# Attention with hashed buckets and two dense layers: value products with 65 weight columns, a host-made projection table, new planner tables

## The chip, the cores and the metric

One core of a Trainium2 chip runs the whole program. The metric is the device time of one execution in microseconds. TensorE does the matrix products (PE in the profile; PEld its weight loads), VectorE is DVE, ScalarE is ACT, GpSimd is POOL, and SyncE (SP) issues nearly all DMA transfers.

## The reference

```python
def _attn_ref(q, k, v, proj):          # 2 x 8 heads, 768 rows, 64 columns
    q_bits, k_bits = (q @ proj > 0), (k @ proj > 0)      # 6 bits each
    mask = q_bucket[:, :, :, None] == k_bucket[:, :, None, :]
    scores = np.where(mask, scale * q @ k.T, -1e9)
    attn = np.exp(scores - scores.max(-1, keepdims=True))
    return (attn / (attn.sum(-1, keepdims=True) + 1e-9)) @ v
x = (1536 tokens, 512)
x = leaky_relu(x @ w_in) @ w_out       # 512 -> 2048 -> 512, slope 0.01
h = x @ w_in2;  out = (h * cos(h)) @ w_out2
```

Everything is float32.

## The kernel before, in words

Products are made in pairs of rounded parts: each operand is split into a high part (a rounded copy, by ScalarE) and a low part (what is left, by a subtraction on POOL or DVE), and high x high, high x low and low x high are summed in PSUM.

There are 16 heads. One head's queries and keys, transposed, stand as a 128 x 768 tile (raw). `hi` and `lo` split it, `bits_mm` (line 277) multiplies it with the signed projection table PB, `bits_wr` (line 283) turns the signs into rows of the tile AT, scaled so that rows of different buckets get a large negative score. `at_dma` copies parts of AT between partitions. `max_mm` (293) forms the scores of 128 rows by 768 at a time, and `max_red` (299) their maximum on DVE; after six of them `row_mm`, `row_fin` and `row_dma` (303 to 313) write the maxima as one more row of AT, beside a row of -1 that `minus_one` loads by DMA (454). `qk` (370, 371) then forms scores that have the maximum already subtracted, `exp` and `exp_cv` (377 to 388) take the exponential on ScalarE and its rounded copy, `exp_lo` (392) subtracts; LO says which of DVE and POOL does it. `pv` (405) multiplies with V, six key blocks, three pairs of parts and two halves of 384 columns, 36 products a head, and `pv_e` (397) opens the sum with two products that add the epsilon and the case of rows without a partner. The old weights are 128 columns: 64 of V and 64 of ones (VH) or zeros (VL), so that 64 rows of the result hold the row sum; even and odd heads share the ones and so have V above or below. `evac` (412) copies the result out, row sums go through a DMA, `recip` (419), a DMA to DRAM and a broadcast back (`lc_dma`, `dr_dma`, `rr_dma`), and `xmul` (430) divides. Every four heads V is loaded (325), split (331, 335), and summed over its rows by products with ones (`sum_v`, 342; 65 weight columns, 256 streamed).

The dense layers (`Moe`, lines 664 to 742) follow: each of two layers takes 48 steps of 12 input and 12 output products of 512 columns; the last four steps divide one output block into two halves of 256 (`columns`, 708). The integer weights are made into two float parts by seven steps per chunk (`Weights.stages`, lines 581 to 592, on ScalarE, DVE and POOL); eight chunks are begun during heads 12 to 15.

The order of nearly all this up to the twelfth dense step is written by a planner (`Plan.order`, line 116). It runs a list of operations in a model of five queues (PE, DVE, ACT, POOL, SP): each has a cost (COST), what it must follow, and a place in a ring of buffers. The queue that can start first takes the operation that can start first there, and among those that could start at the same moment, the one with the least key. The key is the head's position (6 a head) plus KEY of the kind, or FIX of kind and head. CHUNK_KEY does the same for the weight chunks. Program order on each engine is what results. The first loads and constants (lines 209 to 251) stand outside the planner, ahead of it; `zeros` and `v_ones` are two operations of POOL in it. Costs model the duration of each; products before 22 us count 1.9 times as long.

Of the kernel before, what the change touches and what calls it, by code (L numbers as in the profile page):

```python
# [49 lines left out]
}  # L50
CHUNK_KEY = (132.0, 106.0, 116.9, 111.2, 249.3, 102.4, 235.2, 115.5)

COST = dict(
    load=0.5, hi=0.83, d2=0.55, d3=0.55, lo=1.87, dl=0.55, bm=1.06, bw=1.1, db2=0.7, db1=0.55,
    mm=0.351, mr=0.953, rt=0.12, fl=0.55, dr=0.75, de=1.3, neg=0.65, qk=0.702, ex=0.81, cv=0.84, subV=0.95, subG=1.87,
    pe=0.351, pv=0.702, pw=0.351, ev=0.83, lc=0.55, rc=0.18, dw=0.45, rr=0.55, xm=1.85, xh=0.83, xl=1.87,
    vload=0.6, vh=0.83, vl=1.87, sv=1.37, sh=0.75, sl=0.4,
    wload=0.4, w0=1.11, w1=0.69, w2=0.69, w3=1.15, w4=1.15, w5=1.06, w6=2.4,
    hi0=0.52, lo0=0.52, k2=0.83, idt=0.5, bm0=1.0, bw0=0.69, kb0=0.52,
    mi=2.73, ga=0.6, gm=0.68, gh=0.63, glV=0.65, glG=1.3, mo=2.73, ye=0.65,  # L60
)
# [22 lines left out]
BM = 96 + 2 * NB  # L84
# [10 lines left out]
class Plan:  # L95
# [799 lines left out]
```

## Time and profile before

| | us |
|---|---|
| timed runs, median of 3 | 791.51 |
| lowest and highest | 790.81, 791.82 |
| profiled execution, first to last instruction | 789.9 |
| PE busy | 772.2 (98%) |
| DVE, ACT, POOL busy | 472.9, 435.1, 408.9 |

The profiled execution has a span and no separate device time of its own; the timed runs lie 0.9 to 1.9 us above the span. Since products are pipelined, PE's busy time counts a product's record, which overlaps with the next one's, and is no measure of how densely products follow each other. That is read from the distance between starts, or from a merged piece of the chain of waits: its length divided by its count.

### The profile page before, as it was taken

How to read it: one execution, taken by the hardware profiler on the slowest of the kernel's cores; microseconds unless marked ns; L12 is line 12 of the kernel's file. 1: busy time of each engine (PE TensorE's matmuls, PEld its weight loads, DVE VectorE, ACT ScalarE, POOL GpSimd, SP SyncE). 2: the span in 40 equal slices, each digit the busy share in tenths (PEclk: the TensorE clock that was granted, in tenths of full speed). 3: DMA queues.
4: the chain of work that ended last, by engine and by line, in shares of the span. 5: the costliest groups of instructions: out<-in, count | busy, mean ns of one | idle time of the engine just before them, and what ended most of it. 6: DMA issues, size and time to landing. Idle time of an engine off the chain costs nothing.

```text
span 789.9 us, 9962 instructions
## 1 busy us (share of the span) xinstructions
PE 772.2 (98%) x3660; PEld 666.1 (84%) x3660; DVE 472.9 (60%) x599; ACT 435.1 (55%) x630; POOL 408.9 (52%) x263
## 2 busy tenths in 40 slices
PE   5999999999998999999999999999999999999998
PEld 3999999999888888888888888888888888888886
DVE  6656777777597875256366275357546738743333
ACT  3687777877778744243243233366556645644432
POOL 8777675666575634255345346747615433532211
PEclk9999999999999999999999999999999999999999
DMA  6553543542613622032022013112203200000012
GB/s 179 134 129 84 147 96 92 137 104 65 197 32 132 219 107 107 1 107 90 18 107 75 32 54 108 53 41 75 98 1 107 107 1 1 0 1 1 0 54 107
DMA packets 24329, 63.20 MB, mean 80 GB/s; under 512 B 7596, under 2 KB 11620, under 8 KB 20184
## 3 DMA queue, kind: packets, MB, share of 16 engines
q1 hardware_dynamic: 24136, 62.43, 26.0%
q8 instruction: 29, 0.48, 0.3%
q14 instruction: 20, 0.16, 0.1%
q10 hardware_dynamic: 144, 0.13, 0.0%
HBM read 46.21 MB, written 3.19 MB: 63 GB/s over the span
## 4 chain that ended last, share of the span: by engine, by line
PE 92%; DVE 3%; ACT 2%; DMA 2%; issue 1%; POOL 0%; SPq 0%; DVEq 0%; ACTq 0%; POOLq 0%
PE h L664 33%; PE y L706 33%; PE pv L405 11%; PE st L293 4%; PE st L370 4%; PE st L371 4%; PE st L277 2%; PE st L342 1%; DMA raw<-in_qk_dram 1%; PE pv L397 1%; DMA sums<-yx 1%; DVE mx L299 0%; ACT st L385 0%; DVE wsc L591 0%; ACT phi L377 0%
## 5 line engine op out<-in xcount | busy, mean ns | idle before, releaser
L695 POOL TENSOR_TENSOR gl<-gf,gh 128x512 fp32r<-128x512 f32 x88 | 136.2, 1548 | 261.1 <-ACT gh L689 188.7
L706 PE MATMUL y<-gh,at 128*128 128x512 f32 x576 | 177.0, 388 | 0.0
L664 PE MATMUL h<-XH,at 128*128 128x512 f32 x576 | 142.3, 389 | 0.0
L664 PEld LDWEIGHTS h<-XH,at 128*128 128x128 f32 x576 | 108.1, 188 | 22.4
L706 PEld LDWEIGHTS y<-gh,at 128*128 128x128 f32 x576 | 108.0, 188 | 22.4
L299 DVE TENSOR_REDUCE mx<-st 128x1 fp32r<-128x768 f32 x96 | 90.3, 953 | 37.1 <-PE st L293 35.3
L706 PE MATMUL y<-gl,at 128*128 128x512 f32 x288 | 111.8, 388 | 0.0
L392 POOL TENSOR_TENSOR plo<-pf,phi 128x768 fp32r<-128x768 f32 x43 | 81.3, 1894 | 56.1 <-ACT phi L388 49.3
L671 ACT ACTIVATE gf<-h 128x512 f32<-128x512 f32 x48 | 28.7, 597 | 139.8 <-PE h L664 135.8
L681 DVE TENSOR_TENSOR gf<-h,gf 128x512 f32<-128x512 f32 x48 | 33.2, 691 | 108.2 <-ACT gf L671 108.0
L675 ACT ACTIVATE ki<-h 128x512 int32<-128x512 f32 x48 | 28.7, 598 | 105.1 <-PE h L664 105.1
L676 DVE SCALAR_TENSOR_TENSOR gf<-ki,h 128x512 f32<-128x512 int32 x48 | 33.0, 687 | 75.1 <-ACT ki L675 75.1
L664 PE MATMUL h<-XL,at 128*128 128x512 f32 x288 | 77.0, 389 | 0.0
L370 PE MATMUL st<-at 77*128 77x384 f32 x192 | 67.0, 349 | 3.3 <-DVE plo L392 1.3
L371 PE MATMUL st<-at 128*128 128x384 f32 x192 | 65.1, 339 | 0.0
L585 POOL TENSOR_TENSOR at<-wsc,at 128x1024 fp32r<-128x1024 f32 x24 | 59.1, 2462 | 9.6 <-ACT at L592 9.6
L664 PEld LDWEIGHTS h<-XL,at 128*128 128x128 f32 x288 | 54.1, 188 | 11.2
L706 PEld LDWEIGHTS y<-gl,at 128*128 128x128 f32 x288 | 54.0, 188 | 11.1
L689 ACT ACTIVATE gh<-gf 128x512 fp32r<-128x512 f32 x96 | 60.0, 625 | 3.0 <-DVE gf L681 1.5
L706 PE MATMUL y<-gh,wx 128*128 128x512 f32 x192 | 58.7, 387 | 0.0
L685 DVE SCALAR_TENSOR_TENSOR gf<-gf,h 128x512 f32<-128x512 f32 x48 | 32.9, 686 | 41.7 <-ACT gf L684 41.7
L392 DVE TENSOR_TENSOR plo<-st,phi 128x768 fp32r<-128x768 f32 x53 | 50.3, 952 | 10.5 <-ACT st L385 9.1
(105 smaller groups left out, 1452.1 us busy)
## 6 DMA issues: line engine op xcount, KB each, us to landing
wrvh<-in_w_dram SPq DMA_DIRECT2D x16, 1024.0 KB
wrvl<-in_w_dram SPq DMA_DIRECT2D x16, 1024.0 KB
at<-at SPq DMA_DIRECT2D x63, 192.0 KB
raw<-in_qk_dram SPq DMA_DIRECT2D x15, 384.0 KB
vraw<-in_v_dram SPq DMA_DIRECT2D x4, 768.0 KB
yx<-dr SPq DMA_DIRECT2D x16, 192.0 KB
out_dram<-ys SPq DMA_DIRECT2D x6, 256.0 KB
out_dram<-yx SPq DMA_DIRECT2D x5, 256.0 KB
```

What stands on the lines that cost most here:

```text
L299: V.reduce_max(mx[n][:, t:t + 1], mps.pop((n, t))[:, :, 0:HS], axis=AX.XY)
L370: T.matmul(o, at[0:R76 + 1, 2, kc], at[0:R76 + 1, 0, COL[h]], start=True, stop=False)
L371: T.matmul(o, at[:, 3, kc], at[:, 1, COL[h]], start=False, stop=True)
L392: (V if LO[n][k] == "V" else G).tensor_tensor(halves(plo[n, k]), pf.pop((n, k)), halves(f32(phi[n, k])), op=ALU.subtract)
L405: T.matmul(ot[n][:, h, 0:HS], w, x[:, COL[h]], start=False, stop=(k == C - 1 and part == 1))
L585: G.tensor_tensor(lf, sc, f32(hf), op=ALU.subtract)
L664: self.tc.nc.tensor.matmul(ps, w[:, 0, k], x[:, k, cols], start=(j == 0), stop=(j == 3 * KT - 1))
L676: nc.vector.scalar_tensor_tensor(g, ki, -TWOPI, ps, op0=ALU.mult, op1=ALU.add)
L681: nc.vector.tensor_tensor(g, ps, g, op=ALU.max)
L689: self.tc.nc.scalar.activation(gh, self.gs[s], AF.Copy)
L695: (nc.vector if s < GLV else nc.gpsimd).tensor_tensor(gl, g, f32(gh), op=ALU.subtract)
L706: self.tc.nc.tensor.matmul(self.half(e, c), w[:, 1, e], x[:, c], start=(j == 0 and i == 0), stop=(j == GRP - 1 and i == 2))
```

## The change

The weights of a value product are 65 columns (64 of V and one of ones or zeros) for every head, so the row sum is row 64 of the result in every head; SV, the evacuation and the divide follow this layout, and odd heads are divided from partitions 0 to 63 into 64 to 127, with a tile of their own (rr1) for the reciprocals. The projection table is laid out on the host with a table of its signs beside it (128 x 218 values), and both are loaded on ScalarE's queue with the constants; DVE makes PB by three operations. The halves of head 0 become operations of the planner (`ld0`), the first on SP's queue. The row of -1 comes out of the bit write, so `minus_one` goes. The memsets of E and SV move from POOL to DVE. `behind` is new in the planner: the operation may start once the other has started, not ended; the loads of heads use it. Its tables are made anew: 432 entries of FIX for kind and head where there were 49, other costs, keys, and a time that passes between an operation's end and its result (TAIL). In the diff, lines of context and repeated small edits are left out, and the entries of FIX.

```diff
-    load=-181, hi=20, d2=-40, d3=51, lo=-43, dl=-14, bm=-37, bw=7, db2=-47, db1=-61, mm=-8, mr=34, rt=-30,
-    fl=60, neg=1, dr=-74, de=-45, qk=0.72, ex=-7, cv=31, sub=-14, pe=101, pv=39, pw=-4, ev=19, lc=42, rc=40,
-    dw=-34, rr=-34, xm=69, xh=55, xl=-23, vload=71, vh=3, vl=-6, sv=-9, sh=55, sl=-32, wload=94, w0=62, w1=48,
-    w2=-14, w3=49, w4=-27, w5=96, w6=43, mi=4, ga=-51, gm=-35, gh=121, gl=-54, mo=84, ye=-9,
+    load=-1402.5, hi=-438.67, d2=-769.89, d3=-983.25, lo=-187.57, dl=-709.62, bm=-17.82, bw=-521.3, db2=-1419.35,
+    db1=211.01, mm=-7.13, mr=-1162.47, rt=-1.18, fl=-477.39, dr=117.38, de=366.66, qk=1.53, ex=-447.6, cv=-866.91,
+    sub=-567.77, pe=1936.57, pv=585.55, pw=-477.86, ev=-342.96, lc=1443.25, rc=-983.12, dw=-594.71, rr=1500.38,
+    xm=912.21, xh=-1553.48, xl=-197.89, vload=3019.65, vh=1673.03, vl=1768.56, sv=1402.49, sh=1294.13, sl=1341.39,
+    wload=1281.32, w0=-319.38, w1=1137.97, w2=2068.37, w3=552.4, w4=1061.17, w5=950.32, w6=884.09, mi=40.93,
+    ga=153.93, gm=-1034.74, gh=808.61, gl=283.21, mo=-543.31, ye=-455.08,
...
-CHUNK_KEY = (132.0, 106.0, 116.9, 111.2, 249.3, 102.4, 235.2, 115.5)
+CHUNK_KEY = (484.78, 3377.12, -1208.89, 3288.78, 2056.81, -547.14, -95.7, -707.94)
-    load=0.5, hi=0.83, d2=0.55, d3=0.55, lo=1.87, dl=0.55, bm=1.06, bw=1.1, db2=0.7, db1=0.55,
-    mm=0.351, mr=0.953, rt=0.12, fl=0.55, dr=0.75, de=1.3, neg=0.65, qk=0.702, ex=0.81, cv=0.84, subV=0.95, subG=1.87,
-    pe=0.351, pv=0.702, pw=0.351, ev=0.83, lc=0.55, rc=0.18, dw=0.45, rr=0.55, xm=1.85, xh=0.83, xl=1.87,
-    vload=0.6, vh=0.83, vl=1.87, sv=1.37, sh=0.75, sl=0.4,
-    wload=0.4, w0=1.11, w1=0.69, w2=0.69, w3=1.15, w4=1.15, w5=1.06, w6=2.4,
-    hi0=0.52, lo0=0.52, k2=0.83, idt=0.5, bm0=1.0, bw0=0.69, kb0=0.52,
-    mi=2.73, ga=0.6, gm=0.68, gh=0.63, glV=0.65, glG=1.3, mo=2.73, ye=0.65,
+    load=0.6, hi=0.735, d2=0.6, d3=0.6, lo=1.81, dl=0.56, bm=1.053, bw=1.117, db2=0.85, db1=0.58,
+    mm=0.349, mr=0.87, rt=0.06, fl=0.43, dr=0.78, de=1.55, qk=0.704, ex=0.705, cv=0.735, subV=0.875, subG=1.81,
+    pe=0.347, pv=0.683, pw=0.341, ev=0.69, lc=0.6, rc=0.1, dw=0.42, rr=0.56, xm=1.8, xh=0.735, xl=1.8,
+    vload=0.65, vh=0.735, vl=1.8, sv=1.39, sh=0.785, sl=0.45,
+    wload=0.4, w0=1.03, w1=0.6, w2=0.6, w3=1.13, w4=1.13, w5=0.96, w6=2.36,
+    ld0=0.6, hi0=0.58, lo0=0.47, k2=0.735, idt=0.48, bm0=0.53, bw0=0.69, kb0=0.52,
+    mi=2.72, ga=0.495, gm=0.605, gh=0.537, glV=0.602, glG=1.3, mo=2.72, ye=0.55,
-LAT = dict(P=0.06, V=0.04, A=0.04, G=0.1, Q=0.03)
+LAT = dict(P=0.06, V=0.04, A=0.04, G=0.06, Q=0.03)
+TAIL = dict(P=0.16, V=0.09, A=0.1, G=0.05, Q=0.0)
+COLD = 18.0
...
-BM = 96 + 2 * NB
+BM = 96 + 2 * NB + 1
+DV = D + 1
...
-    def add(self, name, e, kind, key, fn, after=(), take=None, give=(), cost=None, moe=False):
+    def add(self, name, e, kind, key, fn, after=(), take=None, give=(), cost=None, moe=False, behind=()):
+        ahead = [self.index[d] for d in behind if d in self.index]
-                  cost=COST[kind] if cost is None else cost, out=[], left=len(deps), moe=moe, before=[], place=0)
+                  cost=COST[kind] if cost is None else cost, out=[], left=len(deps) + len(ahead), moe=moe, before=[], place=0, behind=[], ahead=ahead)
+        for d in ahead:
+            d["behind"].append(it)
...
-            if e == "P" and t < 22:
+            if e == "P" and t < COLD:
...
-            end = t + c
+            for o in it["behind"]:
+                o["left"] -= 1
+                o["at"] = max(o.get("at", 0.0), t)
+                if o["left"] == 0:
+                    ready[o["e"]].append(o)
+            end = t + c + TAIL[e]
-                end = wire + 0.8
+                end = wire + 1.1
...
-                o["at"] = max(o.get("at", 0.0), end + LAT[o["e"]] * (o["e"] != e or e == "Q"))
+                o["at"] = max(o.get("at", 0.0), end + LAT[o["e"]] if e != "P" or o["e"] != e else t + c)
...
-        SV = [con.tile([128, 4, 128], F32R, name=f"sv{i}") for i in range(2)]
-        ring("svt", [128, 2, 2, 64], F32R)
+        SV = [con.tile([128, 4, DV], F32R, name=f"sv{i}") for i in range(2)]
+        ring("svt", [128, 4, D], F32R)
...
-        RR, XX = (YX[:, i * S:(i + 1) * S] for i in (2, 3))
+        RR, XX = [YX[0:64, 2 * S:3 * S], rr1], YX[:, 3 * S:4 * S]
+        raw = {}
+        COL = [slice(h * HS, (h + 1) * HS) for h in range(2)]
+        px = con.tile([128, 2 * BM], F32, name="px")
-        pj = con.tile([128, NB], F32, name="pj")
-        Q.dma_start(pj[0:64], proj)
-        Q.dma_start(pj[64:128], proj)
-        raw = {0: plan.tiles["raw"][0]}
-        COL = [slice(h * HS, (h + 1) * HS) for h in range(2)]
-        for c in COL:
-            Q.dma_start(raw[0][:, c], qkt[0, 0][:, c])
-        Q.dma_start(cs, cst)
+        A.dma_start(px, proj)
+        A.dma_start(cs, cst)
-        ph_ = con.tile([128, NB], F32R, name="ph_")
-        pl_ = con.tile([128, NB], F32, name="pl_")
-        for t in PB:
-            V.memset(f32(t), 0.0)
-        V.tensor_copy(ph_, pj)
-        V.tensor_tensor(pl_, pj, f32(ph_), op=ALU.subtract)
-        for t, p in zip(PB, (f32(ph_), pl_)):
-            for s in range(2):
-                for j in range(2):
-                    rows, c0 = slice(64 * s, 64 * s + 64), 64 + 32 * s + j * NB
-                    V.tensor_scalar(t[rows, c0:c0 + NB], p[rows], 1.0 if s == j else -1.0, None, op0=ALU.mult)
-        neg = con.tile([C, 128], F32, name="neg")
-        G.memset(neg, -1.0)
-        ones = con.tile([128, 65], F32R, name="ones")
+        ones = con.tile([128, DV], F32R, name="ones")
-        def zeros():
+        for i in range(2):
+            V.memset(f32(E[i]), 0.0)
+            V.memset(f32(SV[i]), 0.0)
+        signed = px[:, 0:BM]
+        V.tensor_tensor(signed, signed, px[:, BM:], op=ALU.mult)
+        V.tensor_copy(PB[0], signed)
+        V.tensor_tensor(PB[1], signed, f32(PB[0]), op=ALU.subtract)
+        def constants():
-                G.memset(f32(E[i]), 0.0)
-                G.memset(f32(SV[i]), 0.0)
-                for row, x in ((32, EPS_HI), (96, EPS_LO)):
-                    G.memset(f32(E[i][row:row + 1]), 1.0)
-                    for j in range(4):
-                        G.memset(f32(SV[i][row:row + 1, j, 64 - 64 * (j % 2):128 - 64 * (j % 2)]), x)
-                for j in range(4):
-                    G.memset(f32(SV[i][0:1, j, 64 - 64 * (j % 2):128 - 64 * (j % 2)]), float(S))
-        def v_ones():
-            for i in range(2):
-                G.memset(f32(VH[i][:, :, :, 1]), 1.0)
-                G.memset(f32(VL[i][:, :, :, 1]), 0.0)
+                G.memset(f32(VH[i][:, :, :, D]), 1.0)
+                G.memset(f32(VL[i][:, :, :, D]), 0.0)
+                for row, x in ((0, float(S)), (32, EPS_HI), (96, EPS_LO)):
+                    G.memset(f32(SV[i][row:row + 1, :, D]), x)
+                    if row:
+                        G.memset(f32(E[i][row:row + 1]), 1.0)
...
-            return (t[g % 2][:, :, pr, 0:3:2, :] for t in (VH, VL))
+            return (t[g % 2][:, :, 2 * pr:2 * pr + 2, 0:D] for t in (VH, VL))
...
-                    T.matmul(ps[0:65, 0, 0:256], ones, vs[j][:, c, :, 0:3:2, :], start=(c == 0 and j == 0), stop=(c == C - 1 and j == 1))
+                    T.matmul(ps[0:DV, 0, 0:4 * D], ones, vs[j][:, c, :, 0:D], start=(c == 0 and j == 0), stop=(c == C - 1 and j == 1))
-            ps = svp[g][:, 0, 0:256].rearrange("p (a b d) -> p a b d", a=2, b=2)
-            dst = SV[g % 2].rearrange("p (a b) (c d) -> p a (b c) d", b=2, d=64)[:, :, 0:4:3]
-            return ps, dst
+            return svp[g][:, 0, 0:4 * D].rearrange("p (a d) -> p a d", d=D), SV[g % 2][:, :, 0:D]
...
-                T.matmul(ot[n][:, h, 0:HS], SV[(n // 4) % 2][:, n % 4, :], E[n % 2][:, COL[h]], start=True, stop=False)
+                T.matmul(ot[n][0:DV, h, 0:HS], SV[(n // 4) % 2][:, n % 4, :], E[n % 2][:, COL[h]], start=True, stop=False)
-            g, pr, par = (n // 4) % 2, (n % 4) // 2, n % 2
-            vh, vl = (t[g][:, k, pr].rearrange("p a d -> p (a d)")[:, par * 64:par * 64 + 128] for t in (VH, VL))
+            vh, vl = (t[(n // 4) % 2][:, k, n % 4, :] for t in (VH, VL))
-                    T.matmul(ot[n][:, h, 0:HS], w, x[:, COL[h]], start=False, stop=(k == C - 1 and part == 1))
+                    T.matmul(ot[n][0:DV, h, 0:HS], w, x[:, COL[h]], start=False, stop=(k == C - 1 and part == 1))
-            A.activation(halves(OS[n % 2]), ot.pop(n)[:, :, 0:HS], AF.Copy)
+            A.activation(halves(OS[n % 2][0:DV]), ot.pop(n)[0:DV, :, 0:HS], AF.Copy)
-            lr = 64 if n % 2 == 0 else 0
-            Q.dma_start(LC[:, n % 4], OS[n % 2][lr:lr + 1])
+            Q.dma_start(LC[:, n % 4], OS[n % 2][D:DV])
...
-            r = n % 2 * 64
-            Q.dma_start(RR[r:r + 64], DR[n % 4].to_broadcast([64, S]))
+            Q.dma_start(RR[n % 2], DR[n % 4].to_broadcast([64, S]))
-            rows = L if n % 2 else U
-            G.tensor_tensor(XX[rows], OS[n % 2][rows], RR[rows], op=ALU.mult)
+            G.tensor_tensor(XX[L if n % 2 else U], OS[n % 2][U], RR[n % 2], op=ALU.mult)
...
+        def load0(h):
+            if h == 0:
+                raw[0] = plan.tile("raw")
+            Q.dma_start(raw[0][:, COL[h]], qkt[0, 0][:, COL[h]])
...
-            A.activation(AT[0][64:R76, 2, COL[h]], f32(AT[0][96:BM, 0, COL[h]]), AF.Copy)
-        def minus_one(n):
-            Q.dma_start(f32(AT[n][R76:R76 + 1, 2]), neg)
-        def do(kind, n, e, fn, *args, k=0, j=(), after=(), take=None, give=(), cost=None, key=None):
+            A.activation(AT[0][64:R76 + 1, 2, COL[h]], f32(AT[0][96:BM, 0, COL[h]]), AF.Copy)
+        def do(kind, n, e, fn, *args, k=0, j=(), after=(), take=None, give=(), cost=None, key=None, behind=()):
-            plan.add((kind, n) + tuple(j), e, kind, key, lambda: fn(*args), after, take, give, cost)
+            plan.add((kind, n) + tuple(j), e, kind, key, lambda: fn(*args), after, take, give, cost, behind=behind)
-            plan.add(("hi0", h), "A", "hi0", -40, lambda h=h: hi0(h), take=None if h else "raw")
-            plan.add(("lo0", h), "V", "lo0", -40, lambda h=h: lo0(h), [("hi0", h)], give=[("hi0", 0)] if h else ())
+            plan.add(("ld0", h), "Q", "ld0", h - 400, lambda h=h: load0(h), take=None if h else "raw")
+            plan.add(("hi0", h), "A", "hi0", -40, lambda h=h: hi0(h), [("ld0", h)])
+            plan.add(("lo0", h), "V", "lo0", -40, lambda h=h: lo0(h), [("hi0", h)], give=[("ld0", 0)] if h else ())
...
-        plan.add(("v1", 0), "G", "sub", -23, v_ones, cost=2.9)
-        plan.add(("z", 0), "G", "sub", -19, zeros, cost=7.0)
+        plan.add(("z", 0), "G", "sub", -99, constants, cost=5.0)
-            if n < NR:
-                do("neg", n, "Q", minus_one, n)
-                do("load", n, "Q", load_qk, n, take="raw", after=[("hi0", 0), ("load", n - 1), ("dr", n - 3)])
+                do("load", n, "Q", load_qk, n, take="raw", behind=[("ld0", 1), ("load", n - 1), ("dr", n - 3)])
...
-                    do("vh", n, "A", v_hi, g, pr, j=(pr,), after=[("vload", n), ("pw", n - 5, C - 1), ("sv", n - 8), ("v1", 0)])
+                    do("vh", n, "A", v_hi, g, pr, j=(pr,), after=[("vload", n), ("pw", n - 5, C - 1), ("sv", n - 8), ("z", 0)])
...
-                plan.add((kind, s) + tuple(j), e, kind, key + KEY[kind], lambda: fn(*args), after, take, give, cost, moe=True)
+                plan.add((kind, s) + tuple(j), e, kind, key + FIX.get((kind, s), KEY[kind]), lambda: fn(*args), after, take, give, cost, moe=True)
...
-        VH = [xp.tile([128, C, 2, 3, 64], F32R, name=f"vh{i}", tag=f"vh{i}") for i in range(2)]
-        VL = [xp.tile([128, C, 2, 3, 64], F32R, name=f"vl{i}", tag=f"vl{i}") for i in range(2)]
+        wn = 2 * KT * 128
+        VH, VL = ([xp.tile([128, wn], I64, name=f"{t}{i}", tag=f"{t}{i}").bitcast(F32R)[:, 0:C * 4 * DV].rearrange("p (c h d) -> p c h d", c=C, h=4)
+                   for i in range(2)] for t in ("vh", "vl"))
-        wn = 2 * KT * 128
+        rr1 = xp.tile([64, S], F32, name="rr1")
...
-        plan = Plan(rings, dict(P=5.5, V=5.9, A=4.6, G=4.8, Q=3.6))
+        plan = Plan(rings, dict(P=4.4, V=4.0, A=2.8, G=0.8, Q=0.75))
...
-    ins["proj"] = a["proj"]
+    ins["proj"] = np.zeros((128, 2 * BM), np.float32)
+    for s in range(2):
+        for j in range(2):
+            c0 = 64 + 32 * s + j * NB
+            ins["proj"][64 * s:64 * s + 64, c0:c0 + NB] = a["proj"]
+            ins["proj"][64 * s:64 * s + 64, BM + c0:BM + c0 + NB] = 1.0 if s == j else -1.0
...
-    cst[96:BM, 129] = -BIG
+    cst[96:96 + 2 * NB, 129] = -BIG
+    cst[96 + 2 * NB, 129] = -1.0
...
```

## Rows read from the trace of the kernel before

**Rows 1.** The page: the profiled execution's span.

```profile
span 789.9 us, 9962 instructions
```

**Rows 2.** Busy time by stretch; columns: stretch, length, five engines with counts, granted clock, DMA share, GB/s.

```profile
0.00:25.00 25.00, 16.05 (x51) 11.60 (x51) 15.55 (x30) 8.97 (x13) 17.62 (x45) 1.00 0.66 177
25.00:200.00 175.00, 174.57 (x988) 167.79 (x989) 124.47 (x163) 136.48 (x183) 119.04 (x66) 1.00 0.44 109
200.00:263.68 63.68, 59.09 (x308) 53.91 (x307) 50.69 (x57) 49.70 (x64) 39.86 (x21) 0.97 0.37 119
263.68:786.50 522.82, 522.49 (x2317) 432.84 (x2315) 281.83 (x351) 239.94 (x372) 232.44 (x133) 1.00 0.17 60
...
10.00:15.00 5.00, 4.27 (x11) 2.86 (x11) 3.10 (x5) 1.65 (x3) 3.03 (x10) 1.00 0.98 290
```

**Rows 3.** Chain of waits, merged pieces: start, us, engine, tile, line, products.

```profile
34.34 1.40 PE pv L405 x8
...
57.09 1.05 PE st L277 x6
...
176.21 1.38 PE st L342 x12
...
777.47 0.36 PE h L706 x3
```

**Rows 4.** Groups of instructions, one row per shape: count, busy us, mean ns.

```profile
L405 PE MATMUL pv<-phi,vh 128*128 128x384 f32 x192 | 49.9, 341 | 0.0
...
L397 PE MATMUL pv<-e,sv 128*128 128x384 f32 x32 | 8.9, 362 | 0.7 <-ACT yx L412 0.7
```

**Rows 5.** Timeline of the start: start, us, engine, line, what, count, idle before.

```profile
0.75 1.28 ACT L443 ACT_TABLE_LOAD   x1 [0.75 <-PEq L882]
...
2.00 1.06 SPq L216 DMA_DIRECT2D raw<-in_qk_dram  x2
...
3.59 0.73 POOL L239 MEMSET e<- 128x768 f32 x1
...
4.60 1.13 ACT L443 ACTIVATE at<-raw 128x384 fp32r<-128x384 f32 x2 [2.57 <-DMA raw<-in_qk_dram]
...
5.98 1.09 DVE L230 TENSOR_SCALAR pb<-pl__126 64x6 fp32r<-64x6 f32 x4
...
7.29 1.03 DVE L446 TENSOR_TENSOR at<-raw,at 128x384 fp32r<-128x384 f32 x2
...
8.24 0.45 DVE L465 CAST ident<-cs 128x128 fp32r<-128x128 f32 x1
...
8.90 0.63 SPq L325 DMA_DIRECT2D vraw<-in_v_dram  x1
...
12.14 5.28 DVE L299 TENSOR_REDUCE mx<-st 128x1 fp32r<-128x768 f32 x6 [1.90 <-PE st L293]
...
15.61 3.59 POOL L335 TENSOR_TENSOR vl<-vraw,vh 128x768 fp32r<-128x768 f32 x2 [2.49 <-ACT vh L331]
...
18.46 0.74 SPq L313 DMA_DIRECT2D at<-mt  x1
...
19.75 0.41 PE L342 MATMUL st<-vl,ones 128*65 128x256 f32 x1
...
21.45 0.41 PE L342 MATMUL st<-vl,ones 128*65 128x256 f32 x1
...
23.34 0.34 PE L370 MATMUL st<-at 77*128 77x384 f32 x1
```

**Rows 6.** Timeline of the tail: DVE's weight steps and the product behind them.

```profile
235.94 3.35 DVE L591 SCALAR_TENSOR_TENSOR wsc<-wrvh,wsc 128x1024 int32<-128x1024 int32 x1
...
240.21 0.44 PE L370 MATMUL st<-at 77*128 77x384 f32 x1 [1.32 <-DVE plo L392]
```

**Rows 7.** Busy time by stretch around the drop of the clock in the tail.

```profile
236.00:240.00 4.00, 1.94 (x9) 1.03 (x7) 4.00 (x3) 3.97 (x6) 3.33 (x3) 1.00 0.00 0
240.00:245.00 5.00, 4.79 (x18) 4.79 (x19) 3.39 (x7) 3.41 (x5) 2.75 (x2) 0.66 0.35 112
```

More of the change, by code (lines that the diff above doesn't have):

```diff
@@ L62 @@
-KB = dict(load=393, d2=197, d3=197, dl=197, db2=37, db1=197, dr=3, de=3, neg=3, lc=3, dw=3, rr=197, vload=786, wload=1048)
-INNER = ('hi0 lo0 k2 id bm0 bw0 kb0 neg load hi d2 d3 lo dl bm bw db2 db1 mm mr rt fl dr de qk ex cv sub pe pv pw ev'
-         ' vload vh vl sv sh sl z v1').split()
+    load=0.6, hi=0.735, d2=0.6, d3=0.6, lo=1.81, dl=0.56, bm=1.053, bw=1.117, db2=0.85, db1=0.58,
+    mm=0.349, mr=0.87, rt=0.06, fl=0.43, dr=0.78, de=1.55, qk=0.704, ex=0.705, cv=0.735, subV=0.875, subG=1.81,
@@ new lines @@
+    pe=0.347, pv=0.683, pw=0.341, ev=0.69, lc=0.6, rc=0.1, dw=0.42, rr=0.56, xm=1.8, xh=0.735, xl=1.8,
[3 more added lines that the diff above has]
+    mi=2.72, ga=0.495, gm=0.605, gh=0.537, glV=0.602, glG=1.3, mo=2.72, ye=0.55,
+)
+KB = dict(ld0=110, load=233, d2=197, d3=197, dl=197, db2=37, db1=197, dr=3, de=3, neg=3, lc=3, dw=3, rr=197, vload=467, wload=1048)
@@ L66 @@
+INNER = ('ld0 hi0 lo0 k2 id bm0 bw0 kb0 load hi d2 d3 lo dl bm bw db2 db1 mm mr rt fl dr de qk ex cv sub pe pv pw ev'
+         ' vload vh vl sv sh sl z').split()
 PORT = ('w1', 'w2', 'w3', 'w4', 'glV')
-LAT = dict(P=0.06, V=0.04, A=0.04, G=0.1, Q=0.03)
+LAT = dict(P=0.06, V=0.04, A=0.04, G=0.06, Q=0.03)
+TAIL = dict(P=0.16, V=0.09, A=0.1, G=0.05, Q=0.0)
+COLD = 18.0
 EPS = np.float32(1e-9)
@@ L175, in order, with attention @@
         return done
-def attention(tc, ctx, plan, sums, dr_p, XH, XL, AT, VH, VL, YX, qkt, v, proj, cst, fd, more_raws, heads=NH):
+def attention(tc, ctx, plan, sums, dr_p, XH, XL, AT, VH, VL, YX, rr1, qkt, v, proj, cst, fd, more_raws, heads=NH):
     nc = tc.nc
@@ L489, in attention @@
                 do("bw", n, "V", bits_wr, n, after=[("bm", n), ("d2", n), ("d3", n)], give=[("bm", n)])
-                do("db2", n, "Q", at_dma, n, slice(64, R76), 2, slice(96, BM), 0, after=[("bw", n)])
+                do("db2", n, "Q", at_dma, n, slice(64, R76 + 1), 2, slice(96, BM), 0, after=[("bw", n)])
                 do("db1", n, "Q", at_dma, n, L, 1, U, 0, after=[("bm", n), ("dl", n)])
@@ L510, in attention @@
                 do("qk", n, "P", qk, n, k, k=k, j=(k,), take="st",
-                   after=[("dr", n), ("neg", n), ("d3", n), ("dl", n), ("db1", n), ("db2", n)])
+                   after=[("dr", n), ("d3", n), ("dl", n), ("db1", n), ("db2", n)])
                 if me == "V":
@@ L828, in attn_moe_kernel @@
         rings = dict(raw=2, vraw=1, phi=3, plo=3, pf=2, os=2, r=1, x=1, mx=3, mt=3, svt=1, st=3, pv=1)
-        plan = Plan(rings, dict(P=5.5, V=5.9, A=4.6, G=4.8, Q=3.6))
+        plan = Plan(rings, dict(P=4.4, V=4.0, A=2.8, G=0.8, Q=0.75))
         inner = ExitStack()
-        attention(tc, inner, plan, sums, dr_p, XH, XL, AT, VH, VL, YX, qk, v, proj, cst, fd, lambda: more_raws(0))
+        attention(tc, inner, plan, sums, dr_p, XH, XL, AT, VH, VL, YX, rr1, qk, v, proj, cst, fd, lambda: more_raws(0))
         m = Moe(tc, XH, XL, W, fd, out, YX)
```

95 rows, old and new, of the table FIX are left out of this document.

## The prediction

> **What bounds the kernel now.** I read the page first, for the span [rows 1], then a table by stretch [rows 2]. From 263.68 to 786.50 us, the two dense layers, PE is busy 522.49 of 522.82 us; the change touches no product there, so this stretch stays. What can move is the attention before it, and how its 263.68 us divide needs the price of one product when nothing is waited for. The chain of waits gives it [rows 3]: six bit products (384 columns streamed, 108 weight columns) take 1.05 us and eight value products (384 streamed, 128 weight columns) 1.40 us, so 0.175 us each; twelve V sums (256 streamed, 65 weight columns) take 1.38 us, 0.115 us each. A product's own record is longer (about 341 ns [rows 4]), since products overlap; busy time therefore hides lost time, and I count products instead. In 0 to 25 us there are 51, of which 12 are V sums: 39 x 0.175 + 12 x 0.115 = 8.2 us of work, 16.8 us lost. In 25 to 200: 988, with 36 V sums, 952 x 0.175 + 4.1 = 170.7 us, 4.3 us lost. In 200 to 263.68: 308 x 0.175 = 53.9 us, 9.8 us lost. So the middle is bound by the number of products and their spacing, the start and the tail by what they wait for.
>
> **Value products.** The change cuts their weight columns from 128 to 65 and leaves the streamed columns. There are three groups of 192 and the opening 32 [rows 4]: 608 products, nearly all in the stretch where PE loses almost nothing, so a saving counts whole. The trace of before has no 384-column product with 65 weight columns. The nearest pair streams 256 columns: with 128 weight columns three take 0.36 us, 0.120 each; with 65, 0.115 each [rows 3]. That is 5 ns less, and 608 x 5 ns = 3.0 us. One end is nothing: 108 weight columns space as 128 do, 0.175 [rows 3]. The other end: nine V sums at 20 us start 1.70 us apart over eight steps, 0.2125 each [rows 5], 256 columns at the 1.2 GHz level (the clock column reads 1.00 there, the spacing tells it), so streaming alone is about 0.107 us at 2.4 GHz, and 0.160 for 384; 65 columns keep 0.115 - 0.107 = 0.008 above it, so 0.168 and 608 x 7 ns = 4.2 us. I take 3.0, from the pair that differs in the weight columns alone.
>
> The Trainium skill (TensorE: Matmul & The Clock Gate, "Weight-path perf modes") says that fast weight loading applies only where there are 128 weights and the type isn't FP32; if the old products had it, 65 columns would lose it, and by that the sum would be 7.0 us or less. The trace doesn't bear that out: 108 columns, which the rule excludes too, space as 128 do [rows 3].
>
> **The start.** Before, SP issues two small loads of the projection table, and the first half of head 0 only at 2.00 us [rows 5]; ScalarE begins on it at 4.60. DVE builds the signed tables in tiny pieces until 5.98 + 1.09 = 7.07 us, so head 0's low part begins only at 7.29. After: the halves go out first, at about 0.75 (1.25 us earlier), so ScalarE can begin near 3.4. The table (111 KB) and the constants (65 KB) go out on ScalarE's queue; two issues, each some 0.6 us at the distance of SP's own, and the 1.28 us load of ScalarE's function table fit before 3.4. Should they not, its first copies are late by the issues at most, 1.2 us. What waits behind those issues on ScalarE is head 0's copies alone. The table's extra bytes take about 0.4 us of the wire. DVE then needs three operations on 109 columns, bounded by its 128-column cast at 0.45 us each: from about 3.6 to 4.9, then the low part, which is 2.4 us earlier than 7.29. The four memsets of E and SV that come from POOL (0.73 us each for E there) fit on DVE between 0.85 and the table's landing near 3.5; uncovered they would cost some 2 us. The chain behind the low part (bits, six row maxima from 12.14 to 17.42, the row written by DMA at 18.46, the first score product at 23.34) moves by those 2.4 us.
>
> It can move further. Between 18.46 and 23.34 PE also does the V sums, which wait for POOL's V low parts (15.61 + 3.59 = 19.20), and these for V's load, issued at 8.90 [rows 5]. After, the load of head 1 follows the halves by order and not by their arrival, and V's is next, at about 2.6; the four loads of -1, which SP issued among these, are gone. The bytes up to V's end are 0.39 + 0.39 + 0.18 + 0.79 = 1.75 MB, some 6 us at the 290 GB/s of 10 to 15 us [rows 2], so V is there near 9 us and the V sums lie in PE's idle time before the row of maxima is back. POOL's constants shrink to eight small memsets and four of 0.73 us, over by about 5 us. With the row landed 2.4 us earlier and nothing queued ahead, the first score product could start near 18. The gain is between 1.2 us (only the issue shift arrives) and 6; I take 4.0, nearer the chain I can count than the upper end.
>
> **The new tables.** Keys decide which of the ready operations goes first. The diff shows new keys and costs, not the order that follows, so this term is bounded. The old cost of a row maximum was 0.953 us, where six in a row take 5.28, 0.88 each [rows 5]; the new one is 0.87. So the planner's clock agrees better with the trace, which speaks for less waiting. The tail shows what can be lost or won. One of DVE's weight steps takes 3.35 us from 235.94, and a low part comes only behind it; PE waits for that before 240.21 [rows 6] and is busy for only 1.94 of the 4 us from 236 to 240, 2.1 us lost; then the granted clock averages 0.66 from 240 to 245 [rows 7], falling from the level of 2.4 GHz to that of 1.2 and back, and 5 x 0.34 = 1.7 us go with it. This place costs about 4 us. If the tail lost no more per us than the middle (4.3 / 175), it would keep 1.6 of its 9.8 us: a gain of 8.2. Three more places like this would lose 12. I take a gain of 3.0, a bit less than this one place, and nothing in the middle.
>
> **Edits that cost nothing.** The evacuation has 65 instead of 128 partitions and the same free size; the row of -1 rides in the bit write (45 instead of 44 rows) and its copy (13 instead of 12); the reciprocal rows get a tile of their own. All are off PE, with ScalarE and DVE idle over a fifth of the middle (136.48 and 124.47 of 175 us busy [rows 2]).
>
> **The sum.** 3.0 + 4.0 + 3.0 = 10.0 us off a span of 789.9: 779.9. The three timed runs lie 0.9 to 1.9 us above that span; from their median, 791.51, the forecast is 781.5.
>
> **The rivals.** *No saving per value product:* the 108-column row speaks for it, the 256-column pair against. 791.5 - 7.0 = 784.5. Chance 0.12. *The start is given back:* head 0 is early, but its score products outrun the exponentials of this one head, and PE waits there until head 1 is ready to fill in, where the value term alone and the tables remain. Then 791.5 - 6.0 = 785.5. Against it stands that from 25 us on PE loses next to nothing. Chance 0.10. *Slower:* DVE's weight steps of heads 12 to 15 come ahead of low parts at more places than now. Chunk 2's key is -1208.89, which puts one of its steps ahead of the subtractions, and some other weight steps slip in whenever DVE is free for a moment. Each place costs about 4 us; with no gain from the tables, the value products and the start give 7, so two such places cancel it and three make it 791.5 - 7 + 12 = 796.5. For it speaks that DVE is busy 50.69 of 63.68 us there [rows 2]; against, that most weight keys are far behind those of the softmax. Chance 0.10. *Nothing comes of it:* the old order loses only 4.3 us in the middle, and a new one can lose there the 7 us that the rest gives: 791.5. Chance 0.05.
>
> **How the numbers follow.** The forecast has the remaining 0.63. Its own bounds are 1.2 (start), nothing for the values and a loss of a few us in the tables on one side, 4.2 + 6 + 8.2 = 18.4 on the other. The range 774 to 789 takes in the first two rivals and nearly all of the forecast's own; left out are the slower case, no change, and about 0.05 below 774. A measurement of this kernel can tell 0.2%, 1.6 us, from no change: faster 0.63 + 0.12 + 0.10 = 0.85, same 0.05, slower 0.10.
>
> **What would show it.** Right: chain pieces of six value products at 1.01 to 1.03 us; the first score product near 18 to 19.5 us instead of 23.34; the first dense product near 253.7 instead of 263.68; no half clock in the tail; the dense stretch again 522 to 523 us. Wrong: value products still 0.175 apart; a first score product after 22 us, with PE or POOL waiting for a load that went out later; a stretch after 200 us with more than 10 us lost and DVE weight steps in the chain.

## The result and the profile after

The changed kernel takes 785.4 us (median of four runs, 785.0 to 786.3) beside 791.66 us for the kernel before on the same chip: ratio 0.9914, 95% interval 0.9892 to 0.9935; by the medians 6.3 us less. The forecast was 781.5. The profiled execution took 785.22 us:

```profile
span 782.9 us, 9928 instructions
```

The table by stretch of the changed kernel, columns as in [rows 2]: start, middle, tail and dense layers.

```profile
0.00:25.00 25.00, 17.36 (x53) 12.46 (x53) 17.49 (x27) 8.25 (x12) 10.69 (x22) 1.00 0.71 192
25.00:200.00 175.00, 174.11 (x986) 153.21 (x986) 124.49 (x162) 135.80 (x182) 118.16 (x65) 0.98 0.44 110
200.00:256.76 56.76, 55.52 (x309) 45.97 (x308) 46.28 (x55) 49.56 (x65) 42.61 (x22) 1.00 0.39 126
256.76:779.60 522.84, 522.50 (x2317) 432.83 (x2315) 291.53 (x353) 239.47 (x372) 228.46 (x132) 1.00 0.17 60
```

The two dense layers take 522.84 us where they took 522.82; they begin 6.92 us earlier, at 256.76. Counted as before, at 0.175 us a product and 0.115 a V sum, the start to 25 us loses 25 - 41 x 0.175 - 12 x 0.115 = 16.4 us (before 16.8), the middle 175 - 950 x 0.175 - 36 x 0.115 = 4.6 (4.3), the tail 56.76 - 309 x 0.175 = 2.7 (9.8). So nearly the whole gain lies in the tail. (The V sums now take 0.119 us each, as the next lines show; with that the middle loses 4.5.) The middle is not the same as before, though: its 4.6 us hold a half clock that is new.

First the price of a product. The chain of waits of the changed kernel (start, us, engine, tile, line, products); L478 are the value products, L418 the V sums, L353 the bit products:

```profile
96.15 1.43 PE st L418 x12
...
101.76 1.05 PE pv L478 x6
102.81 1.05 PE st L353 x6
```

Six value products still take 1.05 us, 0.175 each, as six bit products do. Only their weight loads became shorter. Groups by shape (mean ns), weight load and product of the changed kernel:

```profile
L478 PEld LDWEIGHTS pv<-phi,vh 128*65 128x65 f32 x192 | 25.5, 136 | 5.8 <-ACT phi L462 0.8
...
L478 PE MATMUL pv<-phi,vh 128*65 128x384 f32 x192 | 49.2, 337 | 0.5 <-ACT phi L462 0.5
```

and the same weight load of the kernel before:

```profile
L405 PEld LDWEIGHTS pv<-phi,vh 128*128 128x128 f32 x192 | 35.1, 191 | 0.1
```

The start, timeline of the changed kernel (start, us, engine, line, what, count, idle before):

```profile
0.75 0.86 SPq L515 DMA_DIRECT2D raw<-in_qk_dram  x2
...
3.57 1.19 ACT L518 ACTIVATE at<-raw 128x384 fp32r<-128x384 f32 x2 [0.62 <-DMA raw<-in_qk_dram]
...
5.16 1.02 DVE L521 TENSOR_TENSOR at<-raw,at 128x384 fp32r<-128x384 f32 x2
...
8.92 0.86 ACT L407 ACTIVATE vh<-vraw 128x768 fp32r<-128x768 f32 x1 [1.15 <-DMA vraw<-in_v_dram]
...
9.12 1.62 PE L353 MATMUL st<-at,pb 128*109 128x384 f32 x4 [0.97 <-POOL at L339]
9.81 0.52 ACT L526 ACTIVATE at<-at 13x384 fp32r<-13x384 f32 x1
...
10.54 1.49 PE L369 MATMUL st<-at 76*128 76x384 f32 x4
...
17.77 1.09 DVE L359 TENSOR_SCALAR at<-st,cs 45x768 fp32r<-45x768 f32 x1 [0.36 <-PE st L353]
...
18.11 0.41 PE L418 MATMUL st<-vh,ones 128*65 128x256 f32 x1
...
20.68 0.31 PE L379 MATMUL st<-ident,mx 128*6 128x128 f32 x1
...
21.33 0.74 SPq L389 DMA_DIRECT2D at<-mt  x1
...
25.27 0.69 PE L444 MATMUL st<-at 77*128 77x384 f32 x1 [0.15 <-DVE mx L375]
```

Against [rows 5]: the issue is 1.25 us earlier, ScalarE's first copy 1.03, the low part 2.13, and V's load has landed at 8.92. By the count of products the start is level with the one before (53 by 25 us, before 51). Then head 0's lead is lost. ScalarE's last copy of head 0's bits (L526, 9.81) lies behind V's copy, which waits for V's landing at 8.92; PE does head 1's bits at 9.12, ahead of head 0's max products, and waits for POOL there; DVE writes head 1's and head 2's bits between head 0's row maxima; the V sums go ahead of the row of maxima. So this row's DMA is issued at 21.33 instead of 18.46, and the first score product comes at 25.27 instead of 23.34.

The clock behind that, table by stretch of the changed kernel (columns as in [rows 2]):

```profile
22.00:24.00 2.00, 1.26 (x5) 0.59 (x4) 2.00 (x3) 0.00 (x0) 0.00 (x0) 1.00 0.35 68
24.00:26.00 2.00, 1.60 (x5) 1.03 (x5) 2.00 (x3) 0.81 (x1) 0.00 (x0) 0.69 0.50 167
26.00:28.00 2.00, 2.00 (x8) 2.00 (x8) 0.54 (x2) 0.84 (x2) 1.82 (x1) 0.50 1.05 362
28.00:30.00 2.00, 2.00 (x8) 1.82 (x8) 0.96 (x1) 1.77 (x3) 0.15 (x1) 0.50 1.02 259
30.00:32.00 2.00, 2.00 (x10) 1.87 (x9) 0.01 (x1) 0.57 (x2) 2.00 (x2) 0.60 0.14 34
```

From 22 to 24 us PE is busy for 1.26 of 2 us, since it waits for DVE's row maxima of head 1. Then the granted clock falls to 0.50, the 1.2 GHz level, until about 31.6. The lost shares of the four lines from 24 to 32 are 0.31 + 0.50 + 0.50 + 0.40 of 2 us each: 3.4 us. Before, the granted clock of the stretch from 25 to 200 us was 1.00 [rows 2], here it is 0.98.

In the tail the clock stays at 1.00, and PE's waits are small. In the kernel before, DVE's weight steps (tile wsc) stand in the chain three times behind 230 us:

```profile
237.18 2.11 DVE wsc L591
...
256.52 1.97 DVE wsc L589
...
260.17 1.10 DVE wsc L591
```

In the changed kernel's chain from 200 us to the dense layers there is none; DVE still does such steps there (2.00 us at 247.28), but with PE covered. PE's waits there, all of them (us, times, longest):

```profile
PE pv L478 <- DVE plo L466: 0.5, 2, 0.3
PE st L369 <- DVE mx L375: 0.4, 1, 0.4
PE pv L471 <- ACT yx L485: 0.2, 1, 0.2
```

### The profile page after: what moved, and what is told of

The parts are those of the page before. It is cut to its first block, busy times and chain, and to the rows that moved or that the text cites. A ratio compares the mean times of both kernels' runs of the same rounds, so it can differ in the third digit from the quotient of the medians.

```text
span 782.9 us, 9928 instructions
## 1 busy us (share of the span) xinstructions
PE 769.5 (98%) x3660; PEld 644.5 (82%) x3660; DVE 480.1 (61%) x594; ACT 433.1 (55%) x630; POOL 399.9 (51%) x240
## 4 chain that ended last, share of the span: by engine, by line
PE 94%; DVE 2%; DMA 1%; ACT 1%; issue 1%; POOL 0%; SPq 0%; DVEq 0%; ACTq 0%; POOLq 0%
PE h L733 33%; PE y L775 33%; PE pv L478 11%; PE st L369 4%; PE st L444 4%; PE st L445 4%; PE st L353 2%; DVE mx L375 1%; PE st L418 1%; PE pv L471 1%; DMA sums<-yx 1%; DVE plo L466 1%; DMA raw<-in_qk_dram 1%; DVE yx L807 0%; ACT st L459 0%
```

## The experiments

All ratios are to the kernel before, timed on the same chip beside the run, with their 95% intervals. The experiments come from four chips, on which the medians of the kernel before go from 792.35 to 793.28 us: between chips the ratios compare better than the times.

**Value products with 128 columns (e1_wide).** V's tiles keep their layout; each product reads 128 columns from it, so 63 rows of its result belong to other heads and are not used.

```diff
-            vh, vl = (t[(n // 4) % 2][:, k, n % 4, :] for t in (VH, VL))
+            vh, vl = (t[(n // 4) % 2][:, (k * 4 + n % 4) * DV:(k * 4 + n % 4) * DV + 128] for t in VF)
-                    T.matmul(ot[n][0:DV, h, 0:HS], w, x[:, COL[h]], ...
+                    T.matmul(ot[n][0:128, h, 0:HS], w, x[:, COL[h]], ...
```

> The changed kernel with 128 weight columns in the value products again (65 of the head, 63 of what lies behind them), the order of all instructions kept. Theory: a product of 384 streamed columns is as far from the next with 65 as with 128 weight columns, 0.175 us, so the time is that of the changed kernel, 785.4 us within 0.2%. Rival, the prediction's price of 5 ns a product: 608 x 5 ns = 3.0 us more, 788.4.

785.36 us (782.11 to 787.97), ratio 0.9902 (0.9873 to 0.993): that of the changed kernel. Its chain:

```profile
102.20 1.05 PE pv L485 x6
103.25 1.05 PE st L360 x6
```

The same 1.05 us with 128 columns, and the 788.4 us of the expectation's rival lie above the interval (0.993 of 792.53 us is 787.0). From start to start the median distance behind a value product is 174 to 175 ns with 65 columns and 175 to 176 with 128, so at most 2 of the 5 ns are left, and the times don't show them.

**The changed work in the old order (e2_old_tables).** KEY, FIX, CHUNK_KEY, COST, KB, LAT and the cost formulas of the kernel before; layout and loads as changed.

```diff
-COLD = 18.0
+COLD = 22.0
-TAIL = dict(P=0.16, V=0.09, A=0.1, G=0.05, Q=0.0)
+TAIL = dict(P=0.0, V=0.0, A=0.0, G=0.0, Q=0.0)
...
```

> The changed kernel's layout, loads and constants, with the planner's keys, costs and delays of the kernel before. Theory: the new tables carry the gain, in the tail and the middle, so it comes near the kernel before, 789 to 794 us, with 8 us or more lost after 200 us. Rival: layout and loads carry it, 784 to 787.

794.47 us, ratio 1.0013 (0.9988 to 1.0037): nothing is left of the gain. The start and the tail by stretch, then a piece of the tail's chain:

```profile
24.00:32.00 8.00, 8.00 (x30) 7.09 (x31) 4.27 (x5) 5.48 (x8) 3.87 (x3) 0.62 0.52 161
...
200.00:267.05 67.05, 62.32 (x330) 49.76 (x329) 53.23 (x63) 52.26 (x67) 42.34 (x22) 0.97 0.37 114
...
240.00:250.00 10.00, 7.80 (x33) 5.82 (x34) 7.76 (x8) 6.58 (x10) 7.43 (x4) 0.83 0.35 120
```

```profile
240.26 2.46 DVE wsc L579
242.72 0.88 DVE plo L385
...
243.64 0.44 PE st L363
```

The tail loses 67.05 - 330 x 0.175 = 9.3 us, with the place of [rows 6, 7] again: a weight step of DVE ahead of a low part, PE without work, then the lower clock. Its start has a half clock too (0.62 from 24 to 32 us, 3.0 us lost), so that one does not come from the new tables alone; without it the time would be, by estimate, near 791.5, still that of the kernel before.

**The old work in the new order (e3_new_tables_old_work).** The reverse: the kernel before with the new tables and cost formulas.

> The kernel before (old projection table, old loads, 128 weight columns) with the new keys, costs and cost formulas alone. Theory: the keys are an answer to one set of operations and costs; without the new loads and the new start they give another order, not the one of the changed kernel. The planner, with the new costs, lets the dense part of this mixture begin at 263.8 us of its own clock, where it has 249.3 for the changed kernel and 257.0 for the kernel before; on the chip all of these came 6.7 to 8.7 us later, so the first dense product near 271 and a time of 797 to 801. Rival: the tables by themselves carry the gain, whatever the work they order: 784 to 787.

807.98 us, ratio 1.0182 (1.0145 to 1.0218). Worse than expected by 7 us, on the theory's side. Its start, by stretch:

```profile
0.00:34.00 34.00, 22.17 (x61) 15.54 (x62) 19.67 (x34) 9.83 (x14) 19.43 (x46) 1.00 0.61 159
```

PE does only 61 products in 34 us, where the changed kernel does 87 and the kernel before 98. Its tail is worse too: it lasts from 200 to 279.14 us with 376 products, so it loses 79.14 - 376 x 0.175 = 13.3 us, of which 5.1 lie in a stretch at the granted clock 0.50 from 251.5 to 261.7. Neither part gains alone; work and tables do it together.

**Idle products in the gap (e5_fill_gap).** Two products into a bank not yet in use, behind each of head 1's max products 1 to 4.

```diff
+            if n == 1 and t in (1, 2, 3, 4):
+                for h in range(2):
+                    T.matmul(plan.tiles["pv"][0][0:DV, h, 0:HS], ones, AT[0][:, 1, COL[h]], start=True, stop=True)
```

> The changed kernel with two idle products (result never read) behind each of head 1's maximum products 1 to 4, in the gaps in which PE waits for DVE from 22 to 25 us. Theory: the granted clock falls to half at 24.6 because PE was idle for half of the time before; with the gaps filled it stays, the 6.8 us at half clock become 3.4, and 1.5 to 3.4 us of them reach the end: 782.0 to 784.0 us. Rival: the exponentials of head 0 are late in any case, PE waits for them instead, 785.4 within 0.2%.

780.95 us (780.8 to 781.51), ratio 0.9849 (0.982 to 0.9877); 4.45 us under the changed kernel's 785.4, and 4.41 under e1 on its own chip, which does the changed kernel's work in the changed kernel's time. By stretch:

```profile
22.00:24.00 2.00, 2.00 (x11) 1.14 (x9) 2.00 (x4) 0.00 (x0) 0.00 (x0) 1.00 0.43 121
24.00:26.00 2.00, 2.00 (x10) 1.45 (x10) 1.97 (x3) 0.93 (x2) 0.15 (x1) 1.00 0.42 126
26.00:28.00 2.00, 2.00 (x13) 1.92 (x13) 1.03 (x2) 1.95 (x3) 1.68 (x1) 1.00 1.08 378
28.00:30.00 2.00, 2.00 (x14) 1.63 (x14) 0.56 (x3) 2.00 (x4) 1.60 (x1) 1.00 1.04 243
...
34.00:200.00 166.00, 165.70 (x959) 146.46 (x958) 119.72 (x155) 130.93 (x176) 113.55 (x63) 1.00 0.43 106
```

With PE busy through the gap the clock stays at 1.00, and 26 to 30 us hold 27 products instead of 16. The dense layers begin at 252.67, 4.09 us earlier: the 3.4 us of the clock, 0.37 us by which the first score product comes earlier (24.90), and 0.3 us that I can't place. From 34 to 200 us nothing measurable is lost: 923 x 0.175 + 36 x 0.115 = 165.7 of 166 us.

**More idle products (e6_warm_up).** Twelve ahead of all work, four behind head 0's bits, two behind each of head 0's max products, and those of e5.

```diff
+        spin(12)
...
+            if n == 0 or n == 1 and t in (1, 2, 3, 4):
+                spin(2)
```

> The changed kernel with idle products on ones: twelve before the first bit product, four behind the second, two behind each maximum product of head 0 and behind four of head 1. Theory: PE reaches the full clock by about 6 us instead of 20.7 and keeps it; the products on the way to head 0's row of maxima run in half the time, that row comes about 2 us earlier and the half clock at 24.6 goes: 780 to 783 us. Rival 1: the start is bound by DVE and the transfers, and only the half clock's part is won, 782 to 784. Rival 2: the idle products delay the bits, 786 or more.

781.32 us, ratio 0.9852 (0.9827 to 0.9878), that of e5. The row of maxima is out a microsecond earlier (19.53; e5 20.55) and the first score product at 24.13, yet the dense layers begin at 252.52, only 0.15 us earlier than in e5. What a full clock gives the start, a microsecond at the row, does not reach the end.

**The changed kernel once more (e0_changed_again).**

> The changed kernel once more, beside the two others of this call. 785.4 us within 0.3%; the granted clock again at half for some 6 to 7 us between 23 and 32 us. If instead its runs spread by more than the 0.2% of those with the gap filled, the half clock's place varies from run to run.

784.17 us, ratio 0.9875 (0.9845 to 0.9904). Its six runs go from 780.65 to 785.65, with mean clocks from 0.989 to 1.000: so the extent of the half clock varies from run to run. The slowest run has the lowest clock, and the one at 1.000 (781.48) comes near e5; but at 0.995 and 0.996 stand runs from 780.65 to 784.98, so the mean clock alone does not explain the spread. A run of 780.65 us with a mean clock of 0.996 suggests that the half clock is not paid for in full each time; why is open. On this chip the kernel with the gap filled and three more edges (e4, next) takes 780.73, 3.4 us less than these six runs' median.

**Head 0 first (e4_start_order).** e5 with three edges that put head 0's chain ahead of what had overtaken it.

```diff
-                    do("vh", ... ("z", 0)])
+                    do("vh", ... ("z", 0), ("kb0", 1)])
-                do("bm", n, "P", bits_mm, n, after=[("lo", n)], take="st")
+                do("bm", n, "P", bits_mm, n, after=[("lo", n)] + [("mm", 0, C - 1)] * (n == 2), take="st")
-                do("sv", n, "P", sum_v, g, after=[("vl", n, 0), ("vl", n, 1)], take="st")
+                do("sv", n, "P", sum_v, g, after=[("vl", n, 0), ("vl", n, 1), ("rt", 0)], take="st")
```

> The changed kernel with the gap of 22 to 25 us filled as before, and three more dependencies: the copy of head 0's second half of bits ahead of V's first copy, head 2's bit products behind head 0's last maximum product, the V sums behind head 0's row of maxima. Theory: the start's 2 us were lost to other heads' work that went ahead of head 0's chain; the row of maxima comes at 18 to 19 us instead of 20.7 and the first score product 0.5 to 1 us earlier, of which about 0.7 us reach the end: 779.8 to 780.8 us against 780.95 with the gap filled alone. Rival: the whole 2 us of the earlier row reach the end, 778.5 to 779.5. Rival 2: the moved work is missing later, 781 or more.

780.73 us (779.52 to 782.1), ratio 0.9844 (0.982 to 0.9869): not to be told from e5. Timeline:

```profile
18.71 0.31 PE L382 MATMUL st<-ident,mx 128*6 128x128 f32 x1
...
19.01 1.09 DVE L359 TENSOR_SCALAR at<-st,cs 45x768 fp32r<-45x768 f32 x1 [0.62 <-PE st L353]
...
20.13 0.28 DVE L387 TENSOR_SCALAR mt<-st 6x128 f32<-6x128 f32 x1
...
21.04 0.74 SPq L392 DMA_DIRECT2D at<-mt  x1
```

PE has the row 2 us earlier than in the changed kernel, but on DVE head 2's bit write goes first, and the DMA is issued only 0.29 us earlier.

**The row ahead of that write (e9_row_first).**

```diff
-                do("bw", n, "V", bits_wr, n, after=[("bm", n), ("d2", n), ("d3", n)], give=[("bm", n)])
+                do("bw", n, "V", bits_wr, n, after=[("bm", n), ("d2", n), ("d3", n)] + [("fl", 0)] * (n == 2), give=[("bm", n)])
```

> The kernel of e4_start_order with one more edge: head 2's bits are written by DVE only behind head 0's row of maxima. In e4 the row was out of PE at 18.7 but lay behind that write (19.01 to 20.10) on DVE, so that its DMA went out at 21.04. Theory A: the DMA goes out near 19.0, and as the first score product came 3.7 to 4.0 us behind the DMA's issue in every run of the changed order, it comes near 23.0; the two us reach the end, 778.5 to 779.5. Theory B (rival): the score products now wait behind head 1's max products, which PE has ahead of them in the planned order and which go at the pace of DVE's row maxima; head 2's bits are late by what the row gains. The first score product stays at 24 to 25.3 and the time at 780 to 783.

785.6 us (784.53 to 786.1), ratio 0.9904 (0.9876 to 0.9933). Timeline, then the middle by stretch:

```profile
19.45 0.74 SPq L392 DMA_DIRECT2D at<-mt  x1
...
24.90 0.44 PE L447 MATMUL st<-at 77*128 77x384 f32 x1
...
60.66 0.69 PE L474 MATMUL pv<-e,sv 128*65 128x384 f32 x2 [0.63 <-ACT yx L488]
```

```profile
60.00:66.00 6.00, 5.37 (x23) 4.58 (x23) 2.03 (x4) 2.16 (x3) 4.12 (x3) 0.72 0.38 101
...
34.00:200.00 166.00, 164.44 (x933) 142.53 (x931) 118.09 (x154) 126.47 (x171) 110.67 (x61) 0.99 0.42 105
```

and e4's stretch from 60 to 66 us:

```profile
60.00:66.00 6.00, 6.00 (x36) 5.13 (x36) 4.30 (x8) 4.35 (x7) 3.14 (x2) 1.00 0.23 70
```

The row's DMA is issued at 19.45, and the first score product still comes at 24.90: theory B, PE has head 1's max products ahead of it, which go at the pace of DVE. Neither theory saw the time: the one new edge changes PE's order far behind it (against e4's from 27 to 121 us), and 34 to 200 us hold 933 products where e4 and e5 hold 959; 26 x 0.175 = 4.6 us of the 4.9 by which it is behind e4. Half of these 26 are missing in one place: PE waits 0.51 us for a row maximum before 58.94 and 0.63 us for ScalarE before 60.66, the granted clock is 0.50 from 61.0 to 64.4, and 60 to 66 us hold 23 products where e4's hold 36. Here too a half clock follows short waits, and takes 1.7 us.

**V sums with 128 weight columns (e7_wide_sums).**

```diff
-        ones = con.tile([128, DV], F32R, name="ones")
+        ones = con.tile([128, 128], F32R, name="ones")
```

> The changed kernel with 128 instead of 65 weight columns in the 48 V sums (rows that nobody reads); a look at their spacing only. The prediction's price: 0.120 us each at full clock, as the 256-column products of the last steps have it. Theory: weight columns do not set the spacing, 0.115 us as before, and the 5 ns between these two kinds of product come from something else.

785.38 us in a single run; twelve V sums:

```profile
95.88 1.44 PE st L418 x12
```

1.44 us with 128 columns, 1.43 with 65: the columns don't set this spacing either.

**Keys searched anew (e8_robust_plan_a, e8_robust_plan_b).** One key for each operation, on the base of e6 and with COLD at 7.0, chosen by the mean of the planner's time under three sets of costs.

```diff
+        key = OVER[name]
```

> The kernel with idle products from the start on, and keys of the planner searched anew for the mean of three sets of costs (as they are; DVE, POOL and SP 3 to 10% dearer; ScalarE and POOL 5% dearer), where the changed kernel's keys give 306.3, 314.5 and 320.9 us for the twelfth dense step's end and these 306, 309 and 312. Theory: what is left between plan and chip in the tail, some 3 us, comes from orders that hold only if every cost is met; keys that bear dearer costs win 1 to 3 us of the 781.0 with idle products: 778 to 780. Rival: the tail is bound by DVE's and ScalarE's work itself, 780.5 or more.

> The same with the keys of a second search, for which the planner gives 305.5, 308.3 and 311.2. Theory: 778 to 780 us. Rival: 780.5 or more, as above; or the two differ by over 2 us, and the planner's own number does not tell orders apart at this size.

784.51 us (783.34 to 785.63), ratio 0.9893 (0.9872 to 0.9914), and 783.42 (781.18 to 785.85), ratio 0.9883 (0.986 to 0.9907): medians behind those of e5 and e6, though the fastest run of the second (781.18) reaches them. A miss; the rival, 780.5 or more, held. The planner gives these orders a mean that is about 5 us lower (309 and 308.3 for 313.9), and they are slower: at this size its own number does not say which of two orders is faster on the chip.

## Why the prediction was right or wrong

**The sign, and the size to 3.9 us,** came out, with the gain in another place than forecast: 4.0 in the start, 3.0 in the value products and 3.0 in the tables were named; measured, the tail gave 7.1 and the rest together gave nothing. That the total came so near is luck: the tail gave 4.1 more than the 3.0 of the tables, which is about what the start lacked. The first dense product came at 256.76 where 253.7 was named.

**Value products: wrong, 0 instead of 3.0.** The failed step is the price of 5 ns taken "from the pair that differs in the weight columns alone". It doesn't: three dense products of 0.36 us and twelve V sums of 1.38 us [rows 3] also stream operands of different layout, and rounding to 0.01 us leaves 0.36 for three open by 1.7 ns a product either way. e1 (1.05 for six at 128 columns) and e7 (1.44 against 1.43) show that the columns do not set the distance; after the change the V sums take 1.43 instead of 1.38 at the same 65 columns, which no column count explains (their V tiles have another layout now, and e2, with this layout and the old tables, has 1.43 to 1.45 too; the layout was not tried alone). The right row stood there: 108 columns at 0.175, taken only as one end of the bounds. The rival without a saving here held, at 0.12, and its 784.5 is close, though made of other parts. So is 785.5, the price of the rival in which the start is given back; but PE did not wait for exponentials there. The Trainium skill (TensorE: Matmul & The Clock Gate, "Weight-path perf modes") reserves the fast weight load for full widths; here the narrow load is the shorter one, 136 ns against 191, and neither spacing nor time follows it.

**The start: wrong, no gain where 4.0 was forecast.** The steps up to the low part held (2.13 us for the forecast 2.4; the cast of PB took 0.89 us, above the 0.45 that was to bound it, and the two operations beside it 0.27 and 0.28), and V was there at 8.92 for the forecast "near 9". What failed is "The chain behind the low part ... moves by those 2.4 us", and with it the first score product "near 18": it took head 0's chain to stay next in line, while the prediction itself said that the order behind the keys was not known. The V sums did not lie in PE's idle time but ahead of the row, and the first score product came 1.9 us later. The mark set for this, a first score product after 22 us, was met, though for the order's sake and not for a load that went out later. By itself this cost little: the start loses 16.4 us for 16.8 before, and a lead here hardly reaches the end (in e6 a row of maxima a microsecond earlier brings 0.15 us, in e9 an earlier DMA does not bring the score products forward). Its price is the half clock of 3.4 us, which no case of the prediction had. e5 shows it: with the gap filled the changed kernel stands at 780.95, close to the forecast, but by another sum.

**The tables: right in kind, mis-sized.** 3.0 was taken between +8.2 and -12; the tail gave 7.1, near the upper end. Both marks hold: no half clock in the tail, and no weight step of DVE in its chain. "Nothing in the middle" was short by 3: without the half clock's 3.4 us it loses about 4.6 - 3.4 = 1.2 us instead of 4.3. So the new order gave some 3 us there, and the half clock took them back. But "the new tables" are no term of their own: with the old work they lose 1.8% (e3), and the new work with the old tables gains nothing (e2). That e2 has the old tail's place again is shown; which keys remove it was not taken apart.

**The edits that cost nothing** and the dense stretch (522.84 for the forecast 522 to 523) held. The time around the span is 2.3 us where it was 1.6 to 1.9 in the kernel before and 1.8 in e1; this was not looked into.

**A version that beats both** is e5: 780.95 us, 1.5% under the kernel before and 0.4 to 0.6% under the changed one (784.17 in e0, 785.4).

## What to carry to other kernels

Take the price of a product from a row that streams the same operand, not from a pair that differs in one thing only as far as one has looked. Keys tuned for one set of operations belong to it: time a new layout with tables made for it, and count on one added edge undoing part of an order. Where PE waits in short turns just before a long dense stretch, look at the granted clock behind the gap, not only at the gap: eight idle products were worth 3 to 4.5 us here.

## What was not expected of the hardware

A weight load of 65 columns is 55 ns shorter than one of 128 (136 and 191), yet the products stay 0.175 us apart. The half clock's price was larger than the wait ahead of it: PE idled 0.74 us from 22 to 24 us and 0.40 from 24 to 26, and the clock took 3.4 us. And DVE's weight step of one shape takes from 1.22 us (at 227.60) over 2.00 (247.28) to 3.42 (275.81) in the changed kernel, and took 3.35 before [rows 6]; what stretches it was not tried.
